# Softmax-routed experts after attention and a feed-forward block: the last part of the second expert product in two passes of 64 columns, and a fixed order of two engines in the last block's routing

## The chip, the cores and the metric

The kernel runs on one core of a Trainium2 chip. Its time is the device time of one execution in microseconds (us): 699.77 us as the median of three runs (699.66 to 700.07). TensorE (PE; its weight loads are shown as PEld), VectorE (DVE), ScalarE (ACT), GpSimd (POOL) and SyncE (SP) each work through a queue of instructions in order and wait for one another by semaphores. SP issues the DMA transfers, which 16 DMA engines carry out.

## The reference, cut to what matters

The output of a chunked attention becomes x, 3072 tokens of 512 numbers; a feed-forward block makes x (3072, 512) of it; a layer of 8 experts with 4 slots each follows, and its output is the result. The last layer is where the change lies:

```python
x = _attn_ref(...)                       # 24 chunks of 32 tokens, 4 batches, 8 heads
g = s * relu(x @ w_in) ** 2 + b          # w_in (512, 2048)
x = g @ w_out                            # w_out (2048, 512)
logits = x @ phi                         # phi (512, 32): 8 experts, 4 slots each
d = softmax(logits, axis=0)              # over all 3072 tokens
slot_input = d.T @ x                     # (32, 512)
for e in range(8):
    h = relu(slot_input[e] @ w1[e])      # w1[e] (512, 1024)
    slot_out[e] = h @ w2[e]              # w2[e] (1024, 512)
c = softmax(logits, axis=1)              # over the 32 slots
out = c @ slot_out                       # (3072, 512)
```

## The kernel before

The 3072 tokens are worked in six blocks of 512. For each block PE runs 16 steps of the feed-forward block (`mm_h`, `mm_y`), and the attention of the next block and the routing of the block before (`y_logits`, `y_tr`, `slots`) are strewn between these steps by a table (`bg`). Operands of the feed-forward block are split in two fp32r numbers, so each of its products takes three matmuls. For the routing the softmax over all tokens is kept as a running maximum `mrun`, sum `srun` and slot sums `acc`, renormalised block by block.

After the sixth block nothing is left to lay beside the routing, and the rest is a chain of its own, in which PE and SP follow the order in which the code is written, while the order of ACT and DVE is chosen by a scheduler at build time. It has three stages.

- Routing of the last block (L580 to L628). `y_evac` copies the block's output from four PSUM banks (`YB`) to SBUF, `logit_mm` makes the logits in bank 147 (`lb`), DVE takes their maximum (`mj`, then `mrun`, then its negative `nm`), ACT the exponential `ets`; `y_tr` transposes the block's output by four groups of tokens (copied to `x12n`, `x13n` by DVE and ACT in turn), `e_tr` transposes `ets` (to `ees`), `slots_mm` (L351) multiplies them. Beside it the maxima over the four groups of partitions are brought together (`mxr`, L594; `tb`, L598), which gives two factors `ff` and `aa` and two scaled matrices `dmat`. Sixteen small matmuls each (L612, L621) add the old slot sums `acc` and the new ones `ysum` (a half of tile `x11n`) under these factors into bank 145 (`sib`), and the result is spread to `spt` (tile `x10n`), the stationary operand of the first expert product. `c_tr` (L389) transposes routing weights of the first two blocks for the output; they have nothing to do with `spt`.
- First expert product (L641) and the transposes of its result, and the other `c_group`s.
- Second expert product and output (L677 to L757). The 512 output columns are worked in four parts of 128 (`PARTS`). For a part, `w2_mm` does 16 steps (q, ft) of four matmuls (one for each of four experts, each with 32 of the PE's columns for itself), then DVE copies the sum to SBUF (`acc`, L691), `s4_make` multiplies by a selection matrix (L697), ACT scales and splits it (`s`, L698), DVE makes the second half (L699), and with that as stationary operand `out_piece` computes the output: six pieces (512 tokens each) of 128 by 512 for every part (L709), copied from PSUM by ACT (L716) and DVE (L714) in turn, and written by SP in pairs of 512 KB (L721). PE puts the pieces of a part between the steps of the next: two steps, `s4_make`, four steps, then two pieces after each step. Of the third part only two pieces are made there; four are kept back until the fourth part's steps are through. The six pieces of the fourth part come last and are written one by one, 256 KB each (L719).

An fp32 matmul leaves two records in the trace (the sixteen of L612 are 32 there). Names as `w`, `yt`, `x00n` in the last stage are SBUF tiles: weights of w2 first, later the buffers of the output.

Of the kernel before, what the change touches and what calls it, by code (L numbers as in the profile page):

```python
# [15 lines left out]
P = 128  # L16
# [19 lines left out]
def tile_attention_moe_softmoe(  # L36
# [83 lines left out]
    def r32(ap):  # L120
        return ap.bitcast(F32R)
# [211 lines left out]
    def y_tr(tt, b, eng):  # L333
        for dt in range(4):
            pe.transpose(b[:, dt * 128:dt * 128 + 128], ytv(dt)[:, tt * 128:tt * 128 + 128], ident)  # L335
        if eng == "act":
            act.activation(out=yv(tt), in_=b, func=AF.Copy)
        else:
# [144 lines left out]
    with tc.manual_schedule(engines={mybir.EngineType.PE, mybir.EngineType.SP}):  # L483
# [94 lines left out]


        j = NB - 1  # L580
        y_evac(True)
        lb, tb = MB[0], MB[1]
        old, new = mrun[(j + 1) % 2], mrun[j % 2]
        logit_mm(lb)
        L = lb[:, 0:128]
        dve.tensor_reduce(out=st["mj"], in_=L, axis=AX.X, op=ALU.max)
        dve.tensor_tensor(out=new, in0=st["mj"], in1=old, op=ALU.max)
        dve.tensor_scalar(out=st["nm"], in0=new, scalar1=-1.0, scalar2=None, op0=ALU.mult)
        act.activation(out=ets, in_=L, func=AF.Exp, bias=st["nm"], accum_out=st["sj"])
        y_tr(0, HB[0], "dve")  # L590
        y_tr(1, HB[1], "act")
        pe.transpose(tb[0:1, 0:128], new, ident)
        e_tr(YB[2])
        dve.tensor_reduce(out=mxr, in_=tb[0:1, 0:128].rearrange("p (t s) -> p s t", t=4), axis=AX.X, op=ALU.max)  # L594
        y_tr(2, YB[0], "dve")
        y_tr(3, YB[1], "act")
        for t in range(4):
            pe.matmul(tb[32 * t:32 * t + 32, 256:257], lhsT=mxr, rhs=one, start=True, stop=True)  # L598
        top = tb[:, 256:257]
        act.activation(out=st["ff"], in_=top, func=AF.Exp, scale=-1.0, bias=new)  # L600
        act.activation(out=st["aa"], in_=top, func=AF.Exp, scale=-1.0, bias=old)
        for i, k in enumerate(("aa", "ff")):
            dve.tensor_scalar(out=dmat[i], in0=bident[:, 0:32], scalar1=st[k], scalar2=None, op0=ALU.mult)
        sib = HB[0]
        spt = ybuf[0].rearrange("p (t e s) -> p t e s", t=4, e=8)
        pool.memset(ybuf[0], 0.0)
        c_tr(0, HB[1], dve)
        slots_mm(YB[3])
        for dt in range(4):
            for t in range(4):  # L610
                d = 128 * dt + 32 * t
                pe.matmul(sib[32 * t:32 * t + 32, dt * 32:dt * 32 + 32], lhsT=acc[:, d:d + 32], rhs=dmat[0],  # L612
                          start=(dt == 0), stop=False)
        ysum = hl(ybuf[1])[:, 0]
        act.activation(out=ysum[:, 0:256], in_=YB[3][:, 0:256], func=AF.Copy)
        dve.tensor_copy(ysum[:, 256:512], YB[3][:, 256:512])
        act.activation(out=lts, in_=L, func=AF.Copy)
        for dt in range(4):
            for t in range(4):
                d = 128 * dt + 32 * t  # L620
                pe.matmul(sib[32 * t:32 * t + 32, dt * 32:dt * 32 + 32], lhsT=ysum[:, d:d + 32],  # L621
                          rhs=dmat[1], start=False, stop=(dt == 3))
        c_tr(1, YB[2])
        siv = sib[:, 0:128].rearrange("p (t e s) -> p t e s", t=4, e=8)
        act.activation(out=spt[:, :, 0:4, 0:4], in_=siv[:, :, 0:4, :], func=AF.Copy)
        dve.tensor_copy(spt[:, :, 4:8, 4:8], siv[:, :, 4:8, :])
        dve.tensor_scalar(out=st["sj"], in0=st["sj"], scalar1=st["ff"], scalar2=None, op0=ALU.mult)
        dve.scalar_tensor_tensor(out=srun, in0=srun, scalar=st["aa"], in1=st["sj"], op0=ALU.mult, op1=ALU.add)  # L628

        HS = ybuf[1:3]  # L630
        HT = [ybuf[3].rearrange("p (t n) -> p t n", t=8), None]
# [45 lines left out]
        def w2_mm(part, q, fts):  # L677
            width = PARTS[part][1]
            per = 1024 // width
            for ft in fts:  # L680
                fg, t = divmod(ft, per)
                for e in range(4):
                    pe.matmul(OB[part][32 * e:32 * e + 32, 0:width], lhsT=HT[q][:, ft, 32 * e:32 * e + 32],  # L683
                              rhs=emap["w2", part, q, fg, e][:, t * width:t * width + width],
                              start=(q == 0 and ft == 0), stop=(q == 1 and ft == 7))
                if t == per - 1:
                    for e in range(4):
                        e_free(emap["w2", part, q, fg, e])
            if q == 1 and fts[-1] == 7:
                d0 = PARTS[part][0]  # L690
                dve.tensor_copy(osb[:, d0:d0 + width], OB[part][:, 0:width])  # L691

        def s4_make(part):
            d0, width = PARTS[part]
            cols = slice(d0, d0 + width)
            res = SB[part][:, 0:width]
# [6 lines left out]
        obc = [0]  # L703
        stages = []

        def out_piece(part, c, g):
            d0 = PARTS[part][0] + c * 128
            b = OBANK[obc[0] % 4]
            pe.matmul(b, lhsT=r32(s4[:, d0:d0 + 128]), rhs=r32(hl(c4s[g // 2])[:, g % 2]), start=True, stop=True)  # L709
            if obc[0] % 2 == 0:  # L710
                stages.append(hl(eslot.pop(0)))
            dst = stages[-1][:, obc[0] % 2]
            if obc[0] % 2:
# [3 lines left out]
            obc[0] += 1  # L717
            if part == len(PARTS) - 1:
                sp.dma_start(out=out[d0:d0 + 128, 512 * g:512 * g + 512], in_=dst)  # L719
            elif g % 2:  # L720
                sp.dma_start(out=out[d0:d0 + 128, 512 * g - 512:512 * g + 512].rearrange("p (a n) -> p a n", a=2),  # L721
                             in_=stages[-1])

        pieces = [(part, c, g) for part, (_, width) in enumerate(PARTS) for c in range(width // 128)
                  for g in range(NB)]

        def outs(n):
            for _ in range(n):
                out_piece(*pieces.pop(0))

        def part_seq(part):
            return [(part, q, ft) for q in range(2) for ft in range(8)]

        def w2_some(seq, n):
            for _ in range(min(n, len(seq))):
                part, q, ft = seq.pop(0)
                w2_mm(part, q, (ft,))

        seq = part_seq(0)
        w2_some(seq, 8)  # L740
        h_tr(1)
        c_group(5, SB[1])
        w2_some(seq, 8)
        last = len(PARTS) - 1
        for part in range(last):
            seq = part_seq(part + 1)
# [12 lines left out]

# [61 lines left out]
```

## Time and profile before

| | |
|---|---|
| median of three runs | 699.77 us |
| the profiled execution | 699.0 us, of which span 696.9 us |
| PE busy | 678.8 us (97% of the span) |
| DVE, ACT, POOL busy | 359.0, 352.8, 216.9 us |
| chain that ended last | PE 93%, DMA 2%, DVE 2%, ACT 1% |
| granted TensorE clock | 0.992 on the mean |

The span is from the first to the last instruction; some 2.1 us lie around it. The busy share is a mean over the whole program, and 638 of the 697 us are the feed-forward loop, which the change leaves alone. For a change at the end, the chain of waits and the timeline of the last 59 us are to be read.

### The profile page before, as it was taken

To read this page: it belongs to the slowest core of one execution; us is meant where nothing else is said; L and a number is where in the kernel's file an instruction comes from. 1 tells how busy PE (TensorE), PEld (TensorE's weight loads), DVE (VectorE), ACT (ScalarE), POOL (GpSimd) and SP (SyncE) were. 2 spreads that over 40 slices of the span, in tenths; PEclk is the share of its full clock that TensorE was granted. 3 is DMA by queue.
4 is the path that set the end of the run, shared out by engine and by line. 5 is a ranking of instruction groups with operands and counts; after the bars stand their busy time and mean duration, and the time that the engine had idled before them with its cause. 6 is when DMAs were issued, how large, how long until landed. Compare 5 with 4: busy or idle time off the path is not lost.

```text
span 696.9 us, 12513 instructions
## 1 busy us (share of the span) xinstructions
PE 678.8 (97%) x5091; PEld 536.7 (77%) x5091; DVE 359.0 (52%) x651; ACT 352.8 (51%) x628; POOL 216.9 (31%) x178
## 2 busy tenths in 40 slices
PE   6799999999999999999999999999999999999996
PEld 3578888888788888788888788888788888786374
DVE  5699997447534456534445544554553332224233
ACT  4599984554444445445445354545444544444232
POOL 4100000243343434344434334434434444441000
PEclk9899999999999999999999999999999999999998
DMA  8899712702202201211210211120123522527786
GB/s 307 328 407 365 252 47 92 284 21 89 91 5 87 92 31 62 91 40 59 85 68 24 91 63 60 61 88 4 62 74 131 219 91 91 211 91 272 273 336 270
DMA packets 26553, 94.39 MB, mean 135 GB/s; under 512 B 2944, under 2 KB 2944, under 8 KB 26496
## 3 DMA queue, kind: packets, MB, share of 16 engines
q1 hardware_dynamic: 26496, 93.60, 37.0%
q8 instruction: 40, 0.66, 0.4%
q14 instruction: 17, 0.14, 0.1%
HBM read 87.30 MB, written 6.29 MB: 134 GB/s over the span
## 4 chain that ended last, share of the span: by engine, by line
PE 93%; DMA 2%; DVE 2%; ACT 1%; issue 0%; SPq 0%; POOL 0%; DVEq 0%; POOLq 0%; ACTq 0%
PE bank L291 38%; PE bank L271 37%; PE bank L220 4%; PE bank L180 3%; PE bank L683 2%; PE bank L641 2%; PE bank L335 2%; PE bank L206 1%; DMA yt<-vd 1%; DMA k<-kd 1%; PE bank L313 1%; PE bank L709 1%; PE bank L351 1%; PE bank L389 0%; PE bank L660 0%
## 5 line engine op out<-in xcount | busy, mean ns | idle before, releaser
L291 PE MATMUL bank<-g,wo 128*128 128x512 f32 x1152 | 285.2, 396 | 0.0
L271 PE MATMUL bank<-x,wi 128*128 128x512 f32 x1152 | 277.9, 390 | 0.0
L271 PEld LDWEIGHTS bank<-x,wi 128*128 128x128 f32 x1152 | 216.4, 188 | 45.0
L291 PEld LDWEIGHTS bank<-g,wo 128*128 128x128 f32 x1152 | 211.2, 188 | 49.1 <-ACT wi L258 4.2
L278 DVE SCALAR_TENSOR_TENSOR rt<-bank,cons,rt 128x512 f32<-128x512 f32 x96 | 72.0, 750 | 228.8 <-ACT rt L277 228.7
L264 POOL TENSOR_TENSOR wo<-w,wo 128x512 fp32r<-128x512 f32 x80 | 103.2, 1290 | 205.5 <-ACT wo L263 205.5
L259 POOL TENSOR_TENSOR wi<-w,wi 128x512 fp32r<-128x512 f32 x80 | 103.3, 1291 | 190.7 <-ACT wi L258 190.7
L258 ACT ACTIVATE wi<-w 128x512 fp32r<-128x512 f32 x96 | 60.6, 631 | 150.4 <-PE bank L271 147.3
L279 ACT ACTIVATE g<-rt,cons 128x512 fp32r<-128x512 f32 x96 | 69.5, 724 | 41.9 <-DVE rt L278 40.6
L263 ACT ACTIVATE wo<-w 128x512 fp32r<-128x512 f32 x96 | 60.4, 629 | 54.9 <-PE bank L291 54.3
L280 DVE SCALAR_TENSOR_TENSOR g<-rt,cons,g 128x512 fp32r<-128x512 f32 x96 | 72.0, 750 | 27.3 <-ACT g L279 24.7
L277 ACT ACTIVATE rt<-bank 128x512 f32<-128x512 f32 x96 | 55.8, 581 | 4.3 <-PE bank L271 4.2
L196 ACT ACTIVATE ep<-ep 128x512 f32<-128x512 f32 x22 | 13.8, 628 | 29.8 <-DVE ep L195 29.8
L220 PEld LDWEIGHTS bank<-pb,v 128*64 128x64 f32 x704 | 22.3, 138 | 7.8 <-issue 6.7
L180 PEld LDWEIGHTS bank<-k,q 128*64 128x64 f32 x704 | 22.4, 138 | 5.2 <-issue 5.2
L180 PE MATMUL bank<-k,q 128*64 128x64 f32 x704 | 24.6, 223 | 1.4 <-DMA k<-kd 1.4
L220 PE MATMUL bank<-pb,v 128*64 128x64 f32 x704 | 25.3, 225 | 0.0
L197 DVE TENSOR_REDUCE ast<-ep 128x8 f32<-128x512 f32 x22 | 15.1, 685 | 9.4 <-ACT ep L196 9.1
L223 ACT ACTIVATE x<-bank 128x512 fp32r<-128x512 f32 x24 | 14.3, 596 | 7.0 <-PE bank L220 4.6
L224 DVE TENSOR_TENSOR x<-bank,x 128x512 fp32r<-128x512 f32 x24 | 16.6, 690 | 0.4 <-ACT x L223 0.3
L206 PE MATMUL bank<-cons,ep 128*128 128x128 f32 x88 | 13.4, 275 | 3.3 <-POOL ep L200 2.8
L194 DVE TENSOR_REDUCE ast<-bank 128x8 f32<-128x512 f32 x24 | 16.5, 687 | 0.4
(240 smaller groups left out, 543.4 us busy)
## 6 DMA issues: line engine op xcount, KB each, us to landing
sp<-wd SPq DMA_DIRECT2D x22, 512.0 KB, 9.7
k<-kd SPq DMA_DIRECT2D x22, 512.0 KB, 6.2
v<-vd SPq DMA_DIRECT2D x22, 512.0 KB, 3.6
q<-qd SPq DMA_DIRECT2D x20, 512.0 KB, 5.4
w<-e1d SPq DMA_DIRECT2D x10, 512.0 KB, 3.4
out<-w SPq DMA_DIRECT2D x9, 512.0 KB, 4.0
sp<-e1d SPq DMA_DIRECT2D x7, 512.0 KB, 7.8
sp<-e2d SPq DMA_DIRECT2D x7, 512.0 KB, 7.3
```

The source lines that it names most:

```text
L180: pe.matmul(S[64 * par:64 * par + 64, 2 * i + z, :], lhsT=qt[:, c].rearrange("p h n -> p (h n)"), rhs=kt[:, c, :], start=True, stop=True)
L220: pe.matmul(b[64 * h:64 * h + 64, 64 * m:64 * m + 64], lhsT=vt[:, m, h, :], rhs=pb[:, m // 2, m % 2, h].rearrange("p z n -> p (z n)"), sta ...
L258: act.activation(out=r32(t[:, 0]), in_=raw, func=AF.Copy)
L259: (dve if n < NF else pool).tensor_tensor(out=r32(t[:, 1]), in0=raw, in1=t[:, 0], op=ALU.subtract)
L263: act.activation(out=r32(t[:, 0]), in_=raw, func=AF.Copy)
L264: (dve if n < NF else pool).tensor_tensor(out=r32(t[:, 1]), in0=raw, in1=t[:, 0], op=ALU.subtract)
L271: pe.matmul(HB[n % 2], lhsT=r32(w[:, a, kt, :]), rhs=r32(x[:, b]), start=(kt == 0 and i == 0), stop=(kt == 3 and i == 2))
L277: act.activation(out=r, in_=HB[n % 2], func=AF.Relu, scale=1.0 / WSCALE ** 2)
L278: dve.scalar_tensor_tensor(out=t, in0=HB[n % 2], scalar=s_col, in1=r, op0=ALU.mult, op1=ALU.mult)
L279: act.activation(out=r32(g[:, 0]), in_=t, func=AF.Identity, bias=b_col)
L280: dve.scalar_tensor_tensor(out=r32(g[:, 1]), in0=t, scalar=b_col, in1=g[:, 0], op0=ALU.add, op1=ALU.subtract)
L291: pe.matmul(YB[dt], lhsT=r32(w[:, a, dt * 128:dt * 128 + 128]), rhs=r32(g[:, b]), start=(f == 0 and i == 0), stop=(f == NF - 1 and i == 2))
```

## The change

It does four things.

1. `y_evac` copies the fourth bank of the last block's output in two halves of 256 columns, one by ACT and one by DVE, in place of one copy of 512 by ACT.
2. ACT and DVE follow the written order in the last block's routing (`tc.manual_schedule`), and that order is new: `ets` and its transpose ahead of the copy of `x12n`'s second half; the transposed maximum after the transpose of `ets`; `mxr` after DVE's copy of `x13n`; `dmat` for `ff` ahead of `aa`; both `c_tr` after the two groups of small matmuls and the copies to `spt`.
3. The fourth part is worked in two passes of 64 columns (`PASS`), each of 16 steps with four matmuls of 64 columns, each with its own `s4_make`, and with six pieces of 64 by 512. There are thus 30 pieces and five `s4_make` in place of 24 and four.
4. No pieces are kept back: all six of a pass stand between the steps of the next (before a 64-column pass: four steps, `s4_make`, eight steps, then two pieces after each step). Only the six of the last pass stand at the end; only the last two are written one by one, 128 KB each; the pairs of the 64-column passes have 256 KB.

```diff
     def y_evac(halve=False):
         for dt in range(4):
-            if dt % 2 and not (halve and dt == 3):
+            if halve and dt == 3:
+                act.activation(out=ytv(dt)[:, 0:256], in_=YB[dt][:, 0:256], func=AF.Copy, scale=1.0 / WSCALE)
+                dve.tensor_scalar(out=ytv(dt)[:, 256:512], in0=YB[dt][:, 256:512], scalar1=1.0 / WSCALE, scalar2=None,
+                                  op0=ALU.mult)
+            elif dt % 2:
...
+        with tc.manual_schedule(engines={mybir.EngineType.Activation, mybir.EngineType.DVE}):
+            logit_mm(lb)
...
-        OB = [YB[0], YB[1]] * 2
-        SB = [YB[2], YB[3]] * 2
+        OB, SB = [YB[0], YB[1]], [YB[2], YB[3]]
...
+        PASS = [(d0, 128, i) for i, (d0, _) in enumerate(PARTS[:-1])] + [(384, 64, 3), (448, 64, 3)]
+
+        def w2_mm(n, q, ft):
+            d0, width, part = PASS[n]
+            c0 = 128 * ft + d0 - PARTS[part][0]
+            for e in range(4):
+                pe.matmul(OB[n % 2][32 * e:32 * e + 32, 0:width], lhsT=HT[q][:, ft, 32 * e:32 * e + 32],
+                          rhs=emap["w2", part, q, 0, e][:, c0:c0 + width],
+                          start=(q == 0 and ft == 0), stop=(q == 1 and ft == 7))
...
-            if part == len(PARTS) - 1:
-                sp.dma_start(out=out[d0:d0 + 128, 512 * g:512 * g + 512], in_=dst)
+            if k == 6 * len(PASS) - 2 or k == 6 * len(PASS) - 1:
+                sp.dma_start(out=out[d0:d0 + width, 512 * g:512 * g + 512], in_=dst)
...
-            keep = 4 if part == last - 1 else 0
-            w2_some(seq, 2)
-            s4_make(part)
-            w2_some(seq, 4)
-            while sum(1 for p in pieces if p[0] <= part) > keep:
-                outs(2)
+        for n in range(len(PASS) - 1):
+            seq = pass_seq(n + 1)
+            wide = PASS[n + 1][1] == P
+            w2_some(seq, 2 if wide else 4)
+            s4_make(n)
+            w2_some(seq, 4 if wide else 8)
+            while any(p[0] <= n for p in pieces):
+                outs(min(2, sum(1 for p in pieces if p[0] <= n)))
                 w2_some(seq, 1)
             w2_some(seq, 16)
-        outs(2)
-        s4_make(last)
+        s4_make(len(PASS) - 1)
         outs(len(pieces))
```

How the instructions stand now. First ACT from the end of the feed-forward loop to the copy of `x13n`, before (bank 144 is the fourth of the output, 147 holds the logits):

```order
L308 ACTIVATE x11n<-bank_143 128x512
L308 ACTIVATE x11n<-bank_144 128x512
L337 ACTIVATE x12n<-bank_146 128x512
L589 ACTIVATE ets,sj<-bank_147,nm 128x128
L617 ACTIVATE lts<-bank_147 128x128
L343 ACTIVATE ees<-bank_143 128x128
L337 ACTIVATE x13n<-bank_142 128x512
```

and now:

```order
L312 ACTIVATE x11n<-bank_143 128x512
L306 ACTIVATE x11n<-bank_144 128x256
L606 ACTIVATE ets,sj<-bank_147,nm 128x128
L347 ACTIVATE ees<-bank_143 128x128
L610 ACTIVATE x12n<-bank_146 128x512
L341 ACTIVATE x13n<-bank_142 128x512
```

The exponential has moved ahead of the copy of `x12n`, and the copy from bank 144 has half its columns; the other half is DVE's.

Then PE from the combined maximum to the first expert product, before:

```order
L598 MATMUL bank_148<-one,mxr 32x1 x4
L389 MATMUL bank_146<-cons,crow 128x128 x4
L351 MATMUL bank_144<-x12n,ees 32x512 x2
L351 MATMUL bank_144<-x13n,ees 32x512 x2
L612 MATMUL bank_145<-dmat_124,acc 32x32 x16
L621 MATMUL bank_145<-dmat_125,x11n 32x32 x16
L389 MATMUL bank_143<-cons,s_119 128x128 x4
L641 MATMUL bank_141<-sp_110,x10n 32x512
```

and now:

```order
L617 MATMUL bank_148<-one,mxr 32x1 x4
L355 MATMUL bank_144<-x12n,ees 32x512 x2
L355 MATMUL bank_144<-x13n,ees 32x512 x2
L597 MATMUL bank_145<-dmat_124,acc 32x32 x16
L597 MATMUL bank_145<-dmat_125,x11n 32x32 x16
L393 MATMUL bank_146<-cons,crow 128x128 x4
L393 MATMUL bank_143<-cons,s_119 128x128 x4
L646 MATMUL bank_141<-sp_110,x10n 32x512
```

The first `c_tr` (from `crow`) has moved from ahead of the slots product to just ahead of the first expert product.

Last, DVE from the third part's pieces to the end (a row with `acc` is the copy ahead of an `s4_make`), before:

```order
L714 COPY w_71<-bank_146 128x512
L691 COPY acc<-bank_142 128x128
L714 COPY w_72<-bank_148 128x512
L699 SCALAR_TENSOR_TENSOR s_119<-bank_144,tt,s_119 64x128
L714 COPY w_73<-bank_146 128x512
L714 COPY w_74<-bank_148 128x512
L714 COPY yt_105<-bank_146 128x512
L714 COPY yt_106<-bank_148 128x512
```

and now:

```order
L719 COPY w_72<-bank_148 128x512
L719 COPY w_73<-bank_146 128x512
L694 COPY acc<-bank_142 128x64
L702 SCALAR_TENSOR_TENSOR s_119<-bank_144,tt,s_119 64x64
L719 COPY w_74<-bank_148 64x512
L719 COPY yt_105<-bank_146 64x512
L719 COPY yt_106<-bank_148 64x512
L694 COPY acc<-bank_141 128x64
L702 SCALAR_TENSOR_TENSOR s_119<-bank_143,tt,s_119 64x64
L719 COPY y_107<-bank_146 64x512
L719 COPY y_108<-bank_148 64x512
L719 COPY w_75<-bank_146 64x512
```

Both copies to `acc` of the 64-column passes now stand behind the third of three copies of pieces, and a second chain of `acc` and `s` is new.

## Rows read from the trace of the kernel before

**Rows 1.** Windows: length, busy PE, PEld, DVE, ACT, POOL; clock, DMA share, GB/s

```profile
637.98:645.97 7.99, 6.84 (x140) 4.49 (x139) 4.26 (x15) 3.89 (x13) 0.96 (x1) 1.00 0.51 194
...
688.39:691.13 2.74, 2.01 (x6) 1.04 (x6) 2.64 (x4) 1.68 (x3) 0.00 (x0) 1.00 0.86 347
691.13:696.90 5.77, 0.00 (x0) 0.00 (x0) 0.00 (x1) 0.00 (x0) 0.00 (x0) 0.60 0.77 293
```

**Rows 2.** Windows of the last transfers

```profile
688.50:689.00 0.50, 0.50 (x3) 0.38 (x3) 0.50 (x1) 0.07 (x1) 0.00 (x0) 1.00 0.36 147
...
691.00:695.50 4.50, 0.00 (x0) 0.00 (x0) 0.13 (x1) 0.00 (x0) 0.00 (x0) 0.64 1.00 381
695.50:696.00 0.50, 0.00 (x0) 0.00 (x0) 0.00 (x0) 0.00 (x0) 0.00 (x0) 0.50 0.14 49
```

**Rows 3.** Chain of waits, second expert product: start, length, what

```profile
670.58 0.65 PE bank L709 x2
671.23 0.36 PE bank L683 x8
...
682.09 0.47 PE bank L697 x2
682.56 1.01 PE bank L683 x32
683.57 0.66 PE bank L709 x2
684.23 2.32 PE bank L683 x80
...
688.39 0.74 PE bank L709 x2
```

**Rows 4.** Timeline, last part: start, length, engine, line; behind, idle before it

```profile
682.59 0.37 ACT L698 ACTIVATE s<-bank,tt 128x128 fp32r<-128x128 f32 x1 [2.43 <-PE bank L697]
682.99 0.36 DVE L699 SCALAR_TENSOR_TENSOR s<-bank,tt,s 64x128 fp32r<-64x128 f32 x1 [0.98 <-ACT s L698]
683.50 0.73 PE L709 MATMUL bank<-rt1n,s 128*128 128x512 f32 x2
684.27 0.69 DVE L714 COPY w<-bank 128x512 f32<-128x512 f32 x1 [0.92 <-PE bank L709]
688.01 1.44 SPq L721 DMA_DIRECT2D out<-w  x2
691.04 2.65 SPq L719 DMA_DIRECT2D out<-yt  x4
```

**Rows 5.** Chain of waits, routing of the last block

```profile
640.16 0.60 ACT x12n L337
...
641.15 0.33 PE bank L342
...
643.22 0.69 DVE rt1n L392
...
645.12 0.33 PE bank L621 x16
645.45 0.59 PE bank L389 x4
```

**Rows 6.** Timeline, routing of the last block

```profile
637.34 1.28 ACT L308 ACTIVATE x11n<-bank 128x512 f32<-128x512 f32 x2 [0.78 <-PE bank L291]
640.39 0.27 DVE L594 TENSOR_REDUCE mxr<-bank 1x32 f32<-1x128 f32 x1
642.03 0.69 DVE L339 COPY x13n<-bank 128x512 f32<-128x512 f32 x1 [1.37 <-PE bank L335]
643.04 0.62 PE L351 MATMUL bank<-x12n,ees 128*32 128x512 f32 x2
644.22 0.39 ACT L615 ACTIVATE x11n<-bank 128x256 f32<-128x256 f32 x1 [0.53 <-PE bank L351]
644.64 0.42 DVE L616 COPY x11n<-bank 128x256 f32<-128x256 f32 x1
```

More of the change, by code (lines that the diff above doesn't have):

```diff
@@ L337, in y_tr @@
             act.activation(out=yv(tt), in_=b, func=AF.Copy)
-        else:
+        elif eng == "dve":
             dve.tensor_copy(yv(tt), b)
@@ L580, in tile_attention_moe_softmoe @@
         j = NB - 1
-        y_evac(True)
         lb, tb = MB[0], MB[1]
         old, new = mrun[(j + 1) % 2], mrun[j % 2]
[L584 to L600, printed above, removed]
@@ L601, in tile_attention_moe_softmoe @@
-        act.activation(out=st["aa"], in_=top, func=AF.Exp, scale=-1.0, bias=old)
-        for i, k in enumerate(("aa", "ff")):
-            dve.tensor_scalar(out=dmat[i], in0=bident[:, 0:32], scalar1=st[k], scalar2=None, op0=ALU.mult)
+        L, top = lb[:, 0:128], tb[:, 256:257]
         sib = HB[0]
+        siv = sib[:, 0:128].rearrange("p (t e s) -> p t e s", t=4, e=8)
         spt = ybuf[0].rearrange("p (t e s) -> p t e s", t=4, e=8)
-        pool.memset(ybuf[0], 0.0)
-        c_tr(0, HB[1], dve)
@@ L608, in tile_attention_moe_softmoe @@
-        slots_mm(YB[3])
-        for dt in range(4):
-            for t in range(4):
[L611 to L626, printed above, removed]
@@ L627, in tile_attention_moe_softmoe, with add_groups @@
-        dve.tensor_scalar(out=st["sj"], in0=st["sj"], scalar1=st["ff"], scalar2=None, op0=ALU.mult)
-        dve.scalar_tensor_tensor(out=srun, in0=srun, scalar=st["aa"], in1=st["sj"], op0=ALU.mult, op1=ALU.add)
+        ysum = hl(ybuf[1])[:, 0]
+        def add_groups(src, scale, first):
+            for dt in range(4):
+                for t in range(4):
+                    d = 128 * dt + 32 * t
+                    pe.matmul(sib[32 * t:32 * t + 32, dt * 32:dt * 32 + 32], lhsT=src[:, d:d + 32], rhs=scale,
+                              start=(first and dt == 0), stop=(not first and dt == 3))
@@ new lines, in tile_attention_moe_softmoe @@
+        y_evac(True)
+        with tc.manual_schedule(engines={mybir.EngineType.Activation, mybir.EngineType.DVE}):
+            logit_mm(lb)
+            dve.tensor_reduce(out=st["mj"], in_=L, axis=AX.X, op=ALU.max)
+            dve.tensor_tensor(out=new, in0=st["mj"], in1=old, op=ALU.max)
+            dve.tensor_scalar(out=st["nm"], in0=new, scalar1=-1.0, scalar2=None, op0=ALU.mult)
+            act.activation(out=ets, in_=L, func=AF.Exp, bias=st["nm"], accum_out=st["sj"])
+            y_tr(0, HB[0], "dve")
+            y_tr(1, HB[1], None)
+            e_tr(YB[2])
+            act.activation(out=yv(1), in_=HB[1], func=AF.Copy)
+            pe.transpose(tb[0:1, 0:128], new, ident)
+            y_tr(2, YB[0], "dve")
+            dve.tensor_reduce(out=mxr, in_=tb[0:1, 0:128].rearrange("p (t s) -> p s t", t=4), axis=AX.X, op=ALU.max)
+            y_tr(3, YB[1], "act")
+            pool.memset(ybuf[0], 0.0)
+            for t in range(4):
+                pe.matmul(tb[32 * t:32 * t + 32, 256:257], lhsT=mxr, rhs=one, start=True, stop=True)
+            slots_mm(YB[3])
+            act.activation(out=st["ff"], in_=top, func=AF.Exp, scale=-1.0, bias=new)
+            act.activation(out=st["aa"], in_=top, func=AF.Exp, scale=-1.0, bias=old)
+            for i, k in ((1, "ff"), (0, "aa")):
+                dve.tensor_scalar(out=dmat[i], in0=bident[:, 0:32], scalar1=st[k], scalar2=None, op0=ALU.mult)
+            add_groups(acc, dmat[0], True)
+            act.activation(out=ysum[:, 0:256], in_=YB[3][:, 0:256], func=AF.Copy)
+            dve.tensor_copy(ysum[:, 256:512], YB[3][:, 256:512])
+            add_groups(ysum, dmat[1], False)
+            act.activation(out=spt[:, :, 0:4, 0:4], in_=siv[:, :, 0:4, :], func=AF.Copy)
+            dve.tensor_copy(spt[:, :, 4:8, 4:8], siv[:, :, 4:8, :])
+            c_tr(0, HB[1], dve)
+            c_tr(1, YB[2])
+            act.activation(out=lts, in_=L, func=AF.Copy)
+            dve.tensor_scalar(out=st["sj"], in0=st["sj"], scalar1=st["ff"], scalar2=None, op0=ALU.mult)
+            dve.scalar_tensor_tensor(out=srun, in0=srun, scalar=st["aa"], in1=st["sj"], op0=ALU.mult, op1=ALU.add)
@@ L671, in tile_attention_moe_softmoe, with s4_make @@
         w1_quad(1, [lambda kt: c_group(2 + kt, (HB[1], MB[0])[kt % 2])] * 3 + [lambda kt: h_tr(0)])
-        OB = [YB[0], YB[1]] * 2
-        SB = [YB[2], YB[3]] * 2
+        OB, SB = [YB[0], YB[1]], [YB[2], YB[3]]
         OBANK = [HB[0], HB[1], MB[0], MB[1]]
         osb = acc
[L677 to L681, printed above, removed]
-                for e in range(4):
[L683 to L694, printed above, removed]
+        PASS = [(d0, 128, i) for i, (d0, _) in enumerate(PARTS[:-1])] + [(384, 64, 3), (448, 64, 3)]
[6 more added lines that the diff above has]
+                          start=(q == 0 and ft == 0), stop=(q == 1 and ft == 7))
+            if ft == 7 and (n + 1 == len(PASS) or PASS[n + 1][2] != part):
+                for e in range(4):
+                    e_free(emap["w2", part, q, 0, e])
+            if q == 1 and ft == 7:
+                dve.tensor_copy(osb[:, d0:d0 + width], OB[n % 2][:, 0:width])
+        def s4_make(n):
+            d0, width, _ = PASS[n]
             cols = slice(d0, d0 + width)
-            res = SB[part][:, 0:width]
+            res = SB[n % 2][:, 0:width]
             pe.matmul(res, lhsT=selm, rhs=osb[:, cols], start=True, stop=True)
@@ L704, in tile_attention_moe_softmoe, with out_piece @@
         stages = []
[L706 to L710, printed above, removed]
+        def out_piece(n, g):
+            d0, width, _ = PASS[n]
+            k = obc[0]
+            obc[0] += 1
+            b = OBANK[k % 4][0:width]
+            pe.matmul(b, lhsT=r32(s4[:, d0:d0 + width]), rhs=r32(hl(c4s[g // 2])[:, g % 2]), start=True, stop=True)
+            if k % 2 == 0:
                 stages.append(hl(eslot.pop(0)))
-            dst = stages[-1][:, obc[0] % 2]
-            if obc[0] % 2:
+            dst = stages[-1][0:width, k % 2]
+            if k % 2:
                 dve.tensor_copy(dst, b)
@@ L716, in out_piece @@
                 act.activation(out=dst, in_=b, func=AF.Copy)
-            obc[0] += 1
-            if part == len(PARTS) - 1:
-                sp.dma_start(out=out[d0:d0 + 128, 512 * g:512 * g + 512], in_=dst)
+            if k == 6 * len(PASS) - 2 or k == 6 * len(PASS) - 1:
+                sp.dma_start(out=out[d0:d0 + width, 512 * g:512 * g + 512], in_=dst)
             elif g % 2:
[L721 to L725, printed above, removed]
+                sp.dma_start(out=out[d0:d0 + width, 512 * g - 512:512 * g + 512].rearrange("p (a n) -> p a n", a=2),
+                             in_=stages[-1][0:width])
+        pieces = [(n, g) for n in range(len(PASS)) for g in range(NB)]
         def outs(n):
@@ L729, in outs, with pass_seq @@
                 out_piece(*pieces.pop(0))
[L731 to L732 removed]
         def w2_some(seq, n):
             for _ in range(min(n, len(seq))):
[L736 to L739 removed]
+                w2_mm(*seq.pop(0))
+        def pass_seq(n):
+            return [(n, q, ft) for q in range(2) for ft in range(8)]
+        seq = pass_seq(0)
         w2_some(seq, 8)
         h_tr(1)
[L742 removed]
+        c_group(5, YB[3])
         w2_some(seq, 8)
[L744 to L752 removed]
+        for n in range(len(PASS) - 1):
[6 more added lines that the diff above has]
+                outs(min(2, sum(1 for p in pieces if p[0] <= n)))
                 w2_some(seq, 1)
             w2_some(seq, 16)
[L755 to L756 removed]
+        s4_make(len(PASS) - 1)
         outs(len(pieces))
```

## Prediction

> **What bounds the kernel now.** I read first the chain that ended last, then windows by stage, then the timelines of the stages that the change touches. Up to 638 us PE works on the feed-forward loop, which the change leaves alone; what counts is the last 59 us. In the windows [rows 1] PE is busy for 6.84 of the 7.99 us of the last block's routing, so that stage is nearly PE's own. The stage to look at is the end: from 691.13, where the last copy out of PSUM ends, 5.77 us pass with no engine busy, and the DMA engines alone work. They are full from 691.0 to 695.5, at 381 GB/s [rows 2]: the four pieces kept back and the six of the last part, 10 x 256 KB = 2.6 MB, all reach the queue from 688.01 on [rows 4]. So the end is bound by transfers that come late. Before that PE is the chain [rows 3]: matmuls of w2 (L683), pairs of pieces (L709), and nothing else until 686.55; then the wait for the last `s4_make`, under which the kept pieces are made, until 688.39.
>
> The change buys fewer late bytes with more PE work in front of them. The sum has three terms: the routing, PE's way to the first of the last six pieces (before: 688.39), and the way from there to the end (before: 8.51 us).
>
> **The routing.** The logits wait for the last copy out of the fourth bank. Two copies by ACT took 1.28 us [rows 6], 0.6 each. Now it is 256 columns by ACT and 256 by DVE. The trace has just that pair, from one bank, in L615 and L616 [rows 6]: ACT 0.39, and DVE, 0.42, begins 0.03 after ACT's end. So the halves run one after the other, 0.84 in place of 0.60: +0.25. The page "PSUM — Partial Sum Buffer" of the Trainium skill (section "PSUM bank collisions raise a hardware error") gives the reason: two engines must not read one bank at once, and compilers order them. By the rule the split loses 0.25; were the halves side by side it would gain 0.18. The pair in the trace agrees with the rule, and I take the loss.
>
> Against this the exponential no longer stands behind ACT's copy of `x12n`, 0.60 [rows 5]; its transpose, at 641.15 before, comes 0.35 to 0.55 earlier. The slots product then waits for what is last: `mxr` now stands behind DVE's copy of `x13n`, 0.69 + 0.27 + a small product of 0.17 from about 641.5, so 642.6 to 642.7 instead of 643.04 [rows 6]: -0.4. From there the way to the second half of L621 is the same, since the copy `rt1n` (0.69) [rows 5] and `dmat` behind it lay beside the slots product and set the start of L612 alone: 644.7 in place of 645.12. But now both `c_tr` stand between it and the first expert product: eight records in place of the four that took 0.59 [rows 5], +0.44 at 0.11 each. PE is what ends last there: the copies to `spt` are through earlier. So the routing gives 0.0. Bounds: -0.5 if half of the transposes find a gap, +0.4 if the gain at the exponential is lost in waits.
>
> **PE's way to the last pieces.** The price of a 64-column step is not in the trace. With 128 columns four records take 0.109 us: 80 records in 2.32, 32 in 1.01, the difference over 12 fours [rows 3]. With 32 columns 16 records took 0.33 [rows 5], a latency of some 0.2 included, so at most 0.045 for four. So the columns set it, and I take half of 0.109 and a little: 0.056, 0.11 for a step. Bounds: 0.05 and 0.109. Two passes then cost 32 x 0.11 = 3.6 us in place of 16 x 0.218 = 3.5: the matmuls themselves are nearly free of cost. The pieces are not. A pair takes 0.65, and the gap up to the next, with one step of 0.22 in it, 0.36 [rows 3]: the edges between the two kinds cost 0.14, and a pair 0.79 of PE's time. Five more pairs stand ahead of the last six pieces: two of the kept four, that lay under a wait before, and the three of the first 64-column pass.
>
> Step by step, all else as in the chain [rows 3]: the `s4_make` of the third part starts at 682.09 as before, 0.47; eight steps of 64 columns 0.90 + 0.14: 683.60. Pair of 0.66, gap 0.25, pair, gap: the third begins at 685.42. DVE's copy begins 0.70 after its pair (683.57 to 684.27) and takes 0.69 [rows 4], to 686.81; behind it stands the copy to `acc`, 0.22 for 64 columns (an estimate from 0.69 for 512 and 0.42 for 256), to 687.03. PE has done all it may by 686.75 and waits 0.3. Then `s4_make` 0.42, eight steps 1.04: 688.49. Pairs of 0.61 (an estimate: half of the stationary operand is gone), gaps of 0.25: the third begins at 690.21, its copy by DVE ends at 691.55, `acc` at 691.77, where the product starts. From the product of `s4_make` (682.09) to the first piece (683.50 in the timeline) it took 1.41, with ACT 0.37 and DVE 0.36 [rows 4]; 64 columns save some 0.17: 693.0. That is 4.6 after 688.39. Bounds: pairs at the bare streaming of two times 512 columns, 0.45, would take 1.7 off; the wait at the first `acc` overlapped by more work another 0.3.
>
> **From there to the end.** The last six pieces take ACT and DVE as long as before, since a copy costs by its columns, 2.74 [rows 1], less 0.05: 695.7. The first of their pairs is out of PSUM 1.4 after the first piece, at 694.4. A transfer's bytes begin 0.8 after its issue: issued at 688.01 [rows 4], a share of 0.36 in the half microsecond to 689.0 [rows 2]. So bytes run from 695.2. They are 0.79 MB in place of 2.6, 2.06 us at 381 GB/s, to 697.3; the last issue, at 695.9, would have its bytes through at 697.1. After the last bytes (0.14 of the half microsecond from 695.5 [rows 2], so some at 695.7 at the latest) the span went on for 1.2. So it ends at 698.5: 5.5 after the first piece in place of 8.5, -3.0. The 18 pieces of the first three parts have their transfers done before, in stretches where the queue is not full.
>
> **Sum.** 0.0 + 4.6 - 3.0 = +1.6. Span 698.5, and with 2.1 around it 700.6 against 699.0 of the profiled execution. The median of the runs is 0.77 above that one: 699.77 + 1.6 = 701.4 us. The bound of what a measurement can tell from no change, 0.2%, is 1.4 us: the forecast lies at its edge.
>
> **Rivals.**
>
> - Not slower: pieces cost PE only their streaming. Place: the gaps between w2's matmuls and a pair, the edges of 0.14 and the stationary loads. If 64-column matmuls fill these edges, five pairs cost 0.45 and not 0.79, -1.7: 699.7. From 0.47 a pair downward the change is no longer slower. For it: shorter matmuls leave the PE sooner. Against it: the seven pairs in the chain from 670.58 to 683.57 [rows 3] all took 0.65 to 0.67.
> - The routing pays: the first expert product starts as soon as ACT's part of `spt` is there, and the transposes lie in waits: -0.5, 700.9. Against it: PE takes them in the written order, ahead of that product.
> - A 64-column step is no cheaper than one of 128, because the number of matmuls sets the pace. Then 32 steps cost 0.11 more each, +3.4: 704.8. Against it: 16 records of 32 columns within 0.33 [rows 5]. The page "TensorE: Matmul & The Clock Gate" of the Trainium skill (section "Wait — 56ns, not 53.3ns?") states a floor of some 25 ns from start to start however few the columns; eight records would then take 0.20 a step, an estimate of +2.9 for the two passes. The same row speaks against it, as those records belong to four column groups and start closer together.
> - Transfers of 64 rows run at half the rate: 0.79 MB take 4.1 us instead of 2.06: 703.4. No transfer of 64 rows is in the trace of this stage, so this can't be excluded; with those of 128 rows the queue gave 381 GB/s [rows 2] for 256 KB as well.
> - The order of ACT and DVE now written may be much like the scheduler's, so that part 2 of the change does nothing: then the routing keeps the 0.25 and the 0.44 and loses the gain of 0.4: up to +0.7, 702.1.
>
> **Numbers.** Forecast with its own errors (700.7 to 702.1) 0.62; not slower 0.12; the routing pays 0.10; pace of matmuls 0.04; half rate 0.06; no new order 0.06. Slower by over 0.2% (above 701.2): half of the forecast and a bit, the last three: 0.51. Within 0.2%: the rest of the forecast, most of the second and third: 0.43. Faster: a part of the second with the third on top, 0.06. The range for 8 in 10 reaches from the middle of the two good rivals to where the last one ends: 700.0 to 702.4.
>
> **What would show it.** DVE's half copy begins after ACT's; the first expert product starts within 0.3 of 645.97; 64 records of 64 columns take about 0.9; pairs still come 0.9 apart; PE waits about 0.3 for the first 64-column `acc` and over 1.5 for the second; the first of the last six pieces begins near 693; the DMA engines are no longer full up to the end, and between last copy and end lie 2.7 in place of 5.8. Wrong would be: pairs closer than 0.7, a start of the first expert product before 645.6, or a last stretch of transfers longer than 3 us.

## The result, and the profile after

The changed kernel takes 703.6 us (median of 4 runs, 703.26 to 704.59) against 699.92 for the kernel before on the same occasion (4 runs, 699.66 to 700.25): ratio 1.0055, 95% interval 1.0037 to 1.0072, so 3.9 us slower (2.6 to 5.0; the two medians are 3.7 apart). The forecast was slower, but 701.4, with a range up to 702.4. The profiled execution of after took 703.86 us, its span is 701.9.

The two spans can't be subtracted at once. The program up to the last block's routing is the same in all kernels of this study, yet the feed-forward loop ends anywhere between 636.99 and 640.44 us in their thirteen traces: 637.98 in before, 639.20 in after. Where those two part is seen in a window: from 35.50 to 43.00 us the granted clock of TensorE is 0.91 in the mean in before (first row) and 0.73 in after (second row; the columns are length, busy PE, PEld, DVE, ACT and POOL, clock, DMA share, GB/s).

```profile
35.50:43.00 7.50, 7.50 (x60) 5.98 (x58) 6.54 (x13) 7.36 (x14) 0.00 (x0) 0.91 1.03 410
35.50:43.00 7.50, 7.50 (x52) 5.70 (x52) 5.54 (x12) 6.08 (x11) 0.00 (x0) 0.73 1.02 409
```

Both are means over the clock's two levels. It fell to the lower one (0.50, 1.2 GHz) at 33.5 us in before and at 32.8 in after, in both around a microsecond, 32 to 33, in which PE did nothing. PE was busy without a break from 34 us on, and the clock was back at the upper level (1.00, 2.4 GHz) at 36.9 us in before and only at 39.6 in after. From 46 us on, the same matmul of the loop comes 1.16 to 1.18 us later in after all the way. The thirteen traces agree: ahead of 41 us TensorE spends 6.8 us at the lower level in six of them, which end the loop from 636.99 to 638.79, and 10.2 us in the other seven, which end it from 638.99 to 640.44. Why one execution gets more of it, no run shows; what the change touches comes some 600 us later.

So I count from the end of the loop (the first logits product) and cut what follows in three: the routing up to the first w1 product, the way on to the first of the last six pieces, and from there to the end. In windows of after (columns as above):

```profile
639.20:647.29 8.09, 6.92 (x142) 4.85 (x146) 3.95 (x12) 3.63 (x12) 0.96 (x1) 1.00 0.54 197
664.82:694.09 29.27, 27.89 (x687) 19.75 (x678) 12.45 (x24) 10.08 (x19) 0.00 (x0) 1.00 0.77 294
694.09:696.70 2.61, 1.89 (x6) 0.72 (x6) 1.90 (x3) 1.66 (x3) 0.00 (x0) 1.00 0.74 159
696.70:701.90 5.20, 0.00 (x0) 0.00 (x0) 0.00 (x0) 0.00 (x0) 0.00 (x0) 0.66 0.68 147
692.50:696.00 3.50, 2.32 (x8) 1.02 (x8) 1.86 (x5) 1.70 (x4) 0.00 (x0) 1.00 0.95 206
696.00:696.50 0.50, 0.00 (x0) 0.00 (x0) 0.50 (x2) 0.28 (x1) 0.00 (x0) 1.00 0.05 8
696.50:700.50 4.00, 0.00 (x0) 0.00 (x0) 0.20 (x1) 0.00 (x0) 0.00 (x0) 0.73 0.91 196
697.00:700.00 3.00, 0.00 (x0) 0.00 (x0) 0.00 (x0) 0.00 (x0) 0.00 (x0) 0.73 0.94 201
```

The routing is 8.09 us long (before 8.06, up to the start of w1's products in the chain), the way through w2 to the first of the last six pieces 29.27 (before, 663.57 to 688.39: 24.82), and the end 7.81 (before 8.51). The last four rows are the finding. While the first pass's pieces leave (692.50 to 696.00), and again with the last six (697.00 to 700.00), the DMA engines are as good as full, shares 0.95 and 0.94, and yet they move 206 and 201 GB/s; before, full meant 381 [rows 2]. Between the two, from 696.00 to 696.50, they are all but idle (0.05), so the last pieces' bytes did not wait behind the first pass's. They take 4.0 us.

The way through the last part, in the chain of waits of after (start, length, what):

```profile
683.35 0.46 PE bank L700 x2
683.80 1.03 PE bank L687 x64
...
686.66 0.68 PE bank L714 x2
687.34 0.02 issue
687.36 0.69 DVE w L719
688.05 0.14 DVE acc L694
...
691.83 0.12 ACT yt L721
691.96 3.45 DMA out<-yt
695.40 0.00 issue
695.40 0.67 DVE y L719
```

Eight steps of 64 columns take 1.03 with their edge; three pairs later PE waits for DVE's copy and `acc`. Near the end the chain names a transfer of 3.45 us as what the last copies waited for. That is a trap: the timeline shows no idle time of DVE there, and in the code every pair takes a staging tile of its own (`eslot.pop(0)`), so no copy waits for an earlier transfer to `out`.

```profile
694.09 0.67 PE L714 MATMUL bank<-rt1n,s 128*64 128x512 f32 x2 [0.73 <-DVE s L702]
694.57 1.07 ACT L721 ACTIVATE y<-bank 64x512 f32<-64x512 f32 x2 [0.86 <-PE bank L714]
694.80 1.28 DVE L719 COPY y<-bank 64x512 f32<-64x512 f32 x2 [0.76 <-PE bank L714]
695.55 1.10 SPq L725 DMA_DIRECT2D out<-y  x2
696.01 0.68 DVE L719 COPY w<-bank 64x512 f32<-64x512 f32 x1
696.74 1.85 SPq L723 DMA_DIRECT2D out<-w  x2
```

DVE's two copies to `y` run back to back (x2, 1.28), released by PE, as do ACT's (x2, 1.07); the transfer to `out` merely landed in that moment. What is left as the chain at the end is: product of `s4_make`, pairs, copies, issues from 695.55 on, bytes.

### The profile page after: what moved, and what is told of

Same layout as the page of the kernel before. It is cut to its first block, busy times and chain, and to the rows that moved or that the text cites. A ratio compares the mean times of both kernels' runs of the same rounds, so it can differ in the third digit from the quotient of the medians.

```text
span 701.9 us, 12802 instructions
## 1 busy us (share of the span) xinstructions
PE 683.3 (97%) x5227; PEld 539.1 (77%) x5227; DVE 361.8 (52%) x657; ACT 355.2 (51%) x632; POOL 217.3 (31%) x178
## 4 chain that ended last, share of the span: by engine, by line
PE 93%; DMA 3%; DVE 2%; ACT 0%; SPq 0%; issue 0%; POOL 0%; POOLq 0%; ACTq 0%
PE bank L291 38%; PE bank L271 37%; PE bank L220 3%; PE bank L180 3%; PE bank L687 2%; PE bank L646 2%; PE bank L206 2%; DMA yt<-vd 1%; PE bank L339 1%; PE bank L714 1%; PE bank L317 1%; PE bank L355 1%; DMA k<-kd 1%; DMA out<-yt 0%; PE bank L393 0%; PE bank L665 0%
```

## The experiments

All experiments were timed in 5 rounds beside the kernel before; ratios are to before, with their 95% interval. The lengths are read from each kernel's trace (the span to 0.1 us): where one program piece is the same in two kernels, they repeat to 0.05 us or so, while whole runs of before scatter from 697.68 to 702.14.

| kernel | routing | loop's end to first of last six | from there to the end | loop's end to the end | ratio |
|---|---|---|---|---|---|
| before | 8.06 | 50.41 | 8.51 | 58.92 | 1 |
| after | 8.09 | 54.89 | 7.81 | 62.70 | 1.0055 (1.0037 to 1.0072) |
| new end alone | 8.06 | 54.88 | 7.89 | 62.77 | 1.0056 (1.0042 to 1.0071) |
| new routing alone | 8.09 | 50.46 | 8.55 | 59.01 | 1.0000 (0.9990 to 1.0010) |
| twice the bytes | 8.10 | 54.88 | 7.73 | 62.61 | 1.0053 (1.0034 to 1.0072) |
| split transfers | 8.06 | 50.40 | 10.09 | 60.49 | 1.0029 (1.0020 to 1.0038) |
| alternate halves | 8.09 | 55.12 | 7.19 | 62.31 | 1.0045 (1.0032 to 1.0058) |
| nothing kept back | 8.06 | 51.97 | 7.39 | 59.36 | 1.0003 (0.9993 to 1.0014) |
| two passes, 128 rows | 8.06 | 52.47 | 7.42 | 59.89 | 1.0032 (1.0020 to 1.0044) |
| two kept back | 8.05 | 51.22 | 7.59 | 58.81 | 0.9996 (0.9986 to 1.0006) |
| new version | 7.22 | 50.52 | 7.42 | 57.94 | 0.9985 (0.9974 to 0.9996) |
| new version, splits later | 7.21 | 50.47 | 7.44 | 57.91 | 0.9988 (0.9974 to 1.0001) |

**The change in two halves.** The end of after with the routing of before, and the routing of after with the end of before.

> The kernel before with only the second half of the change: last part in two passes of 64 columns, nothing kept back; the routing as before. Theory A (the loss is all in the end: more PE work ahead of the last six pieces, +4.4 us, and transfers of 64 rows that leave at half the rate, so that the way from the first of these pieces to the end gives back 0.7 us where 3.0 were forecast): 3.6 us slower than before, ratio 1.0052. Rival B (part of the loss comes from the new order in the routing, or from what lies ahead of it): 2.4 us or less, ratio 1.0035 or less.

> The kernel after with the end of before: the new routing alone. Theory A: the way from the end of the feed-forward loop to the first expert product is 8.1 us against 8.0, ratio 1.0001, within 0.1% of before. Rival B: the routing carries 1.2 us of the loss, ratio 1.0017; then the feed-forward loop would end at 639.2 us here too and not at 638.0, or the first expert product would begin over 9 us after it.

The end alone is as slow as after, the routing alone is before again. Theory A holds for both, and the end of the loop at 636.99 in the second, with the new routing in it, shows that the later end in after does not come of the routing.

**128 rows by a pair in one tile.**

```diff
-            b = OBANK[k % 4][0:width]
+            r0 = 64 if narrow and k % 2 else 0
...
+            b = bank[r0:r0 + width]
...
+                sp.dma_start(out=out[d0:d0 + width, 512 * g - 512:512 * g + 512].rearrange("r (h n) -> h r n", h=2),
+                             in_=stages[-1][:, 0])
```

> The kernel after, but the two pieces of a pair of 64 rows stand in the lower and the upper 64 partitions of one staging tile and leave in one transfer of 128 rows by 2 KB (the odd piece is multiplied with 128 stationary columns, of which the upper 64 are its own). Copies, bytes and pairs are the same. Theory A (64 rows move at half the rate: 205 GB/s with packets of 4 KB at 311 ns in the trace of after, against 160 ns with 128 rows): the last stretch of transfers runs at 380 to 400 GB/s, the last six pieces end about 2.4 us earlier, ratio to before 1.002. Rival B (the end is late because the last copy waits for a staging tile whose transfer has to land, 3.45 us in the chain of after, or because issues come 0.6 us apart): no gain, ratio 1.0055.

Neither: 727.74 us, ratio 1.0399 (1.0383 to 1.0415). The window of its last transfers:

```profile
696.00:722.00 26.00, 0.00 (x0) 0.00 (x0) 0.00 (x0) 0.00 (x0) 0.00 (x0) 0.56 0.13 51
```

A share of 0.13 of 16 engines is what two engines give that are busy all the time, at 51 GB/s. The side in memory had an outermost dimension of 2 (`h`); that this set the number of engines fits, but no run tests it. The run says nothing on 64 rows; the next does.

**Twice the bytes.** The kernel after, but the first pass sends nothing and the last six pieces take all 128 columns.

```diff
+            if n == len(PASS) - 1:
+                d0, width = 384, 128
...
-            elif g % 2:
+            elif g % 2 and n != 3:
```

> The kernel after, but the pieces of the first pass of 64 columns are made and copied and not sent; the last six are multiplied with all 128 columns of the last part and leave with 128 rows, in the same form (two pairs and two single pieces). PE's way to them is the same; the late bytes are twice as many, 1.57 MB in place of 0.79, and the transfers have 128 rows in place of 64. Theory A (64 rows move at half the rate): twice the bytes take the same time, 4.1 us at 381 GB/s against 4.05 at 194; the way from the first of the last six pieces to the end is 7.6 to 8.0 us against 7.81, ratio to before 1.0055. Rival B (the end of after was long for another reason, and 64 rows move as fast as 128): 2 us more for the bytes, 9.8 us, ratio 1.008.

```profile
696.81:701.80 4.99, 0.00 (x0) 0.00 (x0) 0.00 (x1) 0.00 (x0) 0.00 (x0) 0.67 0.72 282
697.00:700.00 3.00, 0.00 (x0) 0.00 (x0) 0.00 (x0) 0.00 (x0) 0.00 (x0) 0.76 0.99 391
```

Twice the bytes, the same time: 7.73 us against 7.81, at 391 GB/s against 201 in the same window of after. The ratio's interval, 1.0034 to 1.0072, leaves out B's 1.008. Nor did the end merely follow the issues, which are alike in both kernels: after's engines were not idle between them, but 0.94 busy with half the bytes. Theory A, shown.

**64 rows in before.**

```diff
-                sp.dma_start(out=out[d0:d0 + 128, 512 * g:512 * g + 512], in_=dst)
+                for h in range(2 if g % 2 else 0):
+                    sp.dma_start(out=out[d0 + 64 * h:d0 + 64 * h + 64, 512 * g - 512:512 * g + 512]
+                                 .rearrange("p (a n) -> p a n", a=2), in_=stages[-1][64 * h:64 * h + 64])
```

> The kernel before, where only the way out of the last six pieces is changed: three pairs, each leaving in two transfers of 64 rows by 4 KB, the lower 64 partitions and then the upper 64, in place of six transfers of 128 rows by 2 KB. Bytes, number of transfers and issues are the same; a pair waits for its second copy, which costs 0.35 us at most. Theory A (a transfer from 64 partitions moves at half the rate, and one from the other half behind it in the queue does not help): 1.57 MB at 205 GB/s take 7.7 us in place of 4.1, the kernel is 3 to 4 us slower, ratio 1.005. Rival B (two transfers from different halves run side by side and fill the rate together, or the half rate in after came of something else): 0.4 us slower at most, ratio 1.0006.

```profile
693.50:694.00 0.50, 0.00 (x0) 0.00 (x0) 0.00 (x0) 0.00 (x0) 0.00 (x0) 1.00 0.87 164
694.00:698.50 4.50, 0.00 (x0) 0.00 (x0) 0.00 (x0) 0.00 (x0) 0.00 (x0) 0.65 0.87 294
```

The end is 1.58 us longer than before, between the theories. While only the first lower half was under way, by the order of issues and landings, it moved 164 GB/s (0.87 of the engines busy); in the window after that, lower and upper halves in turn, 294. So a 64-row transfer is slow by itself, and one from the other half does fill some of the gap. Theory A was wrong in that.

**Alternate halves in after.**

```diff
+            r0 = 64 if width < P and k // 2 % 2 else 0
+            pe.matmul(OBANK[k % 4][0:r0 + width], lhsT=r32(s4[:, d0 - r0:d0 + width]),
...
+            b = OBANK[k % 4][r0:r0 + width]
...
+                             in_=stages[-1][r0:r0 + width])
```

> The kernel after, where the pairs of 64-row pieces stand alternately in the lower and the upper 64 partitions (those in the upper half are multiplied with 128 stationary columns, of which the upper 64 are their own); transfers, sizes and issues are the same. Theory A (a transfer of 64 rows moves at half the rate when it is alone, and one from the other half fills the other half of the rate while both are under way, as packets of 160 to 200 ns in the run with split transfers suggest): the last six pieces' bytes take 2.8 us in place of 4.0, the end comes 0.8 to 1.3 us earlier, ratio to before 1.004. Rival B (transfers are served one after the other whichever half they come from, or the end follows the issues): no gain against after, ratio 1.0055, and packets of 4 KB stay at 311 ns.

```profile
696.50:697.50 1.00, 0.00 (x0) 0.00 (x0) 0.24 (x1) 0.00 (x0) 0.00 (x0) 1.00 0.97 201
697.50:699.50 2.00, 0.00 (x0) 0.00 (x0) 0.00 (x0) 0.00 (x0) 0.00 (x0) 1.00 0.90 263
```

The first microsecond, which is the first pair's, goes at 201 GB/s, the two after it at 263, and the end is 0.62 us shorter than in after; the pieces come 0.23 later, so 0.39 remains. The mechanism is A's, its size at most half of what A gave; the intervals of the two ratios, 1.0045 and 1.0055, overlap, so the gain is read from the trace alone. It also rules out that after's low rate came of the size or the number of its transfers, which are the same here.

**The other parts of the end.** Nothing kept back (`keep = 0`, and no pair ahead of the last `s4_make`), and then also two passes, but the six pieces made once with 128 rows.

> The kernel before, one pass of 128 columns as it was, but with no pieces kept back: this part of the change alone. Theory A: two pairs more on PE's way (0.8 and 0.65 us) and 1.05 MB less at the end: the first of the last six pieces 1.45 us later, the way from there to the end 7.5 us in place of 8.5; 0.45 us slower, ratio 1.0006. Rival B: it is the missing kept pieces that cost most of the change's loss (PE idle in the wait for the last product): 2 us or more, ratio 1.003.

> The kernel before with nothing kept back and the last part of w2 in two passes of 64 columns, but its six pieces made once, with 128 rows, after the second pass (the first pass has no s4_make and no pieces of its own). Theory A: the passes themselves cost next to nothing, since 64 columns take half of 128: 0.2 us over the kernel without kept pieces, 0.65 us over before, ratio 1.0009; so the loss of the change is in the six extra half-height pieces on PE's way with their wait (2.9 us) and in the 64-row transfers. Rival B: the passes of 64 columns are what costs, 1.5 us or more over the kernel without kept pieces.

Without kept pieces the trace gives +0.44 (59.36 against 58.92), as A said. The two passes add 0.53, where A gave 0.2. Of that 0.28 is a stretch in which PE waited for nothing that the profile shows, in the chain of that kernel (after's chain has no such stretch):

```profile
686.80 1.90 PE bank L682 x122
688.71 0.28 issue
688.98 0.56 PE bank L682 x22
...
691.18 0.75 PE bank L713 x2
```

Timed, it is more: 1.4 to 3.1 us over before against 0.97 in the trace, and by the medians 1.9 us over the kernel without kept pieces, which is B's number. About 0.7 of that lies outside the span: 2.5 to 2.9 us of each of its five executions do, in the other kernels about 2 (after: 1.9). With it the trace gives some 1.6 over before, inside the interval. Of the thirteen traces this alone has a transfer of instructions (16 KB, 1.3 us) behind the end of the span; whether the 0.7 us come of it, no run shows. They are no part of the loss in after.

**A better version.** Two pieces kept back; then the routing of after with a whole fourth copy, the transposes of c4 in PE's waits and another order of y's copies; then the same with two `c_split` written later.

```diff
-            keep = 4 if part == last - 1 else 0
+            keep = 2 if part == last - 1 else 0
...
+            c_tr(0, HB[1], dve)
             slots_mm(YB[3])
...
+            for tt in range(4):
+                pe.transpose(YB[2][:, tt * 128:tt * 128 + 128], crows[1][:, tt].rearrange("p r s -> p (r s)"), ident)
             add_groups(ysum, dmat[1], False)
```

> The kernel before with two pieces of the third part kept back in place of four (one pass of 128 columns, transfers of 128 rows). Theory A: the first of the last six pieces comes 0.85 us later (one pair more on PE's way), the late bytes are 0.52 MB fewer (1.37 us at 381 GB/s), so the end comes 0.5 us earlier, ratio 0.9993. Rival B: the DMA engines were not the bound of the end; it follows PE's last pieces, 0.85 us later, ratio 1.0012.

> A version against both: the routing of after with three edits, and the end of before with two pieces kept back. The edits: the last copy of the fourth bank is whole again (ACT alone, -0.25); the transposes of the first two rows of c4 lie in PE's waits, ahead of the slots product and between the two groups products (-0.6); the third transpose of y is ahead of that of the exponential, and its copy and that of the fourth go to DVE with the reduction of the maximum between them (-0.4). Theory A: the way from the end of the feed-forward loop to the first expert product is 6.8 us in place of 8.06, and the end as with two pieces kept (-0.1): 1.3 us faster than before, ratio 0.998. Rival B: the copies for c4 that now come early on DVE push back its half of the slots copy, and the first expert product waits for the second half of spt: 7.5 us or more, ratio 0.999 or above.

> The version that was 0.15% faster than before, with the splits of the third and fourth row blocks written behind the copies to spt on ACT and DVE (0.51 us of them stood ahead of the first copy to spt). Theory A: the first expert product begins 6.8 to 6.9 us after the end of the feed-forward loop in place of 7.22, all else as in that version: 1.3 us faster than before, ratio 0.998. Rival B: the split is late for the transposes in the second half of w1, which then wait: 7.2 us or a longer way through w1, ratio 0.9985 or above.

Two kept back gain 0.1 in the trace, not 0.5. PE's way is 0.81 longer, as A said (0.85), but the end is only 0.92 shorter and not 1.37. In this kernel the DMA engines run short of work before the last six pieces' bytes come:

```profile
692.00:692.25 0.25, 0.22 (x1) 0.00 (x0) 0.25 (x1) 0.25 (x1) 0.00 (x0) 1.00 0.22 82
```

So those six alone set the end, and fewer kept bytes ahead of them save little more (0.2 us at the end with nothing kept back). The new routing takes 7.22 us, between the theories, and the version is 0.98 us shorter in the trace, ratio 0.9985: faster than before by 0.04 to 0.26%, and in the trace 4.76 us shorter than after from the loop's end on. In its chain the logits are back at 1.11, and four transposes lie between the groups products (L624):

```profile
637.76 1.11 PE bank L313 x32
638.88 1.48 PE bank L335 x12
...
642.20 1.00 PE bank L351 x8
643.19 0.32 PE bank L593 x30
643.51 0.60 PE bank L624 x4
...
644.71 0.23 ACT x10n L626
644.94 0.04 issue
644.98 7.07 PE bank L644 x64
```

ACT's 0.51 us of `c_split` ahead of `spt` looked like the next wait. Written later, they gain nothing (7.21): PE's second groups product ends 6.8 us after the loop's end in both, and the copy to `spt` waits for that, not for ACT. B's number came, but not for its reason: the way through w1 is no longer than it was.

## Why the prediction was wrong

**The routing: right, in each term.** Forecast 0.0, measured +0.03. The chain of after:

```profile
639.20 1.37 PE bank L317 x32
...
641.87 0.33 PE bank L346
...
643.95 1.07 PE bank L355 x8
...
645.93 0.33 PE bank L597 x16
646.26 1.02 PE bank L393 x8
647.29 7.00 PE bank L646 x64
```

Counted from the loop's end, against [rows 5, 6]: the logits +0.26 (forecast +0.25), the exponential's transpose -0.50 (-0.35 to -0.55), the slots product -0.38 (-0.4), the second half of L597 -0.41 (-0.42), both `c_tr` 1.02 in place of 0.59, +0.43 (+0.44). And the halves of the fourth bank's copy did run one after the other, DVE 0.03 after ACT's end:

```profile
639.23 0.39 ACT L306 ACTIVATE x11n<-bank 128x256 f32<-128x256 f32 x1
...
639.65 0.42 DVE L307 TENSOR_SCALAR x11n<-bank 128x256 f32<-128x256 f32 x1 [1.11 <-ACT x11n L306]
```

**PE's way: right.** Forecast +4.6 us, measured 29.27 - 24.82 = +4.45. With 1.26 us of shift (third `s4_make` at 683.35 in place of 682.09), the third pair was forecast for 686.68 and came at 686.66, the first wait ended at 688.24 as forecast for 688.29, the last piece came at 694.09 against 694.26. Only the waits were shorter than the signs said: PE stood 0.11 us for the first 64-column `acc` (0.3 forecast) and 0.55 + 0.73 for the second chain (over 1.5). The rivals on the price of a pair and of a 64-column step fall: pairs took 0.61 to 0.68 with gaps of 0.25, eight steps 1.03.

**From there to the end: wrong, by 2.3 us.** The step that failed is "They are 0.79 MB in place of 2.6, 2.06 us at 381 GB/s". The rate of 128-row transfers does not hold for 64 rows: the 0.79 MB took 4.0 us (196 to 201 GB/s), as long as 1.57 MB take with 128 rows in the run with twice the bytes. That is 1.9 of the 2.3 us; the bytes began 2.4 us after the first piece in place of 2.2, and 1.4 us in place of 1.2 followed the last of them. The end shrank by 0.70 in place of 3.0, and the sign that the prediction had named, a last stretch of transfers longer than 3 us, came. This was the fourth rival, at 0.06, and its 703.4 is within 0.2 us of the measured time. I had dismissed it for want of a row; a missing row is no evidence, and the chance should have been that of an open question, which the range then had to reach. (The range ends at 702.4, while the last rival, at which it is said to end, ends at 702.1; either is short of 703.4.)

The page "SBUF — State Buffer" of the Trainium skill (section "Door 1: The DMA port swizzle (why `[64,N]` ≈ `[32,N]`)") states the rule that the prediction did without: the rate follows the ports that the partitions reach, and partitions 0 to 63 reach half of them; it gives 196 GB/s for them, measured there with 1 MiB. The trace of after agrees, with 201 to 206. The page's section "Can I just issue two DMAs to hit both halves?" says no, with a gain of 6%. The runs here differ: with transfers from both halves under way 263 and 294 GB/s.

**The sum.** Routing +0.03, way +4.45, end -0.70, and nothing in w1's stretch between the first two (17.53 us in both): +3.78 in the trace; timed, +3.9 with its interval from 2.6 to 5.0. By parts of the change: nothing kept back +0.44, the two passes +0.53, and the first pass's own pieces and wait with 64-row transfers +2.78 (62.70 - 59.89, less 0.03 of routing), of which 2.39 lie on PE's way and 0.39 at the end. Where the 0.28 us stretch is left out, the two passes count 0.25 and the last part 3.06.

## What to carry to other kernels

Before making late output smaller, see along which axis: halving the rows (SBUF partitions) of a transfer halved its rate too and bought nothing, while the six pieces more cost PE nearly as much as full ones (0.61 a pair against 0.66). A rival that only a missing row speaks against keeps the chance of an open question. And where whole runs scatter by more than the effect, compare the lengths of stages within traces, from an event that both kernels share.

## What the runs showed of the hardware

- Transfers from the lower 64 partitions: 201 to 206 GB/s with the DMA engines 0.94 to 0.97 busy; from all 128: 381 to 391 at the end. With transfers from the lower and the upper half in turn: 263 to 294.
- A transfer whose memory side begins with a dimension of 2 kept 0.13 of the 16 engines busy, at 51 GB/s, and made the kernel 28 us slower (one kernel).
- The same program's feed-forward loop ended between 636.99 and 640.44 us, and the order follows the time that TensorE spent at its lower clock (1.2 GHz) in the first 41 us: 6.8 us in the six earliest, 10.2 us in the seven latest.
